# A third buffer for gate rows, earlier weight loads with one staging tile less, and splits behind the activations, in a fused attention, MLP and mixture-of-experts kernel

## The chip, the cores and the metric

The kernel runs on one core of a Trainium2 chip. The metric is the time of one execution in microseconds (us) of device time; several runs are taken and their median is what counts. The engines are named as in the profile: PE (TensorE, matmuls), PEld (its weight loads), DVE (VectorE), ACT (ScalarE), POOL (GpSimd) and SP (SyncE, which here issues nearly all DMAs, in the order of its own queue).

## The reference

Three stages follow each other. Attention over 8 batches and 8 heads, with 576 queries and with keys and values averaged in groups of 8, so that 72 are left. A dense MLP over the 4608 tokens. A mixture of 8 experts in which each token goes to the one expert with the largest logit.

```
k_p = mean of 8 neighbouring k;  v_p = mean of 8 neighbouring v
x = softmax(q @ k_p.T / sqrt(64)) @ v_p              # 4608 tokens x 512
x = ELU(x @ w_in) @ w_out                            # 512 -> 2048 -> 512
e = argmax(x @ w_gate);  g = softmax(x @ w_gate)[e]
out[token] = g * (relu(x @ w1[e]) @ w2[e])           # 512 -> 1024 -> 512
```

## The kernel before, in words

**Precision.** Every large product is made of three matmuls on fp32 values that are rounded to a high part (`xh`, `wih`, `gh`, `m1h`) and a remainder (`xl`, `wil`, `gl`, `m1l`). Whatever goes into a matmul is therefore first *split*: ACT casts the high part, DVE subtracts it (`split`, L118 to L120; `w_hi` L232 and `w_lo` L235 for the weights of the dense MLP).

**First stage.** Tokens stand in 12 blocks of 384 (three tiles of 128). The list `steps` holds one step for each block and each of 16 pieces of the 2048 inner columns; blocks 0 and 1 are interleaved at the start. `step(n)` issues the first product of its piece (`g1_mm`, L449, tile `h`), its ELU (ACT at L459 to L461, DVE at L466 and L467, then the split into `gh` on ACT at L473 and `gl` on DVE at L474), and the second product of an earlier piece (`g2`, L491, tiles `y`). Between these it runs named slots ("pre", "pe_mid", "dve_first", "bits", "act_end", "end" and others), which calls of `at(n, slot, function, ...)` have filled: attention of later blocks (`sp` L377, `mx` L386, softmax L395 to L401, transposes `aTp` L407 and their copies `aT` L413, `pv` L422, its split `xh`/`xl` L435/436), the pooling of keys and values on DVE (`kT`, `v` at L282), the weights of the dense MLP (bits of the mantissa L215 to L221, then `w_hi`, `w_lo`). This program order is also each engine's order. A few pieces at the start are on POOL: `w_lo` of the second and third weight chunks, and half of the pooling of the second batch's keys (`prep_k_pool`). Ten matmuls on a tile of zeros (`warm`, L279) stand in step 1.

**Gate logits.** For a finished block, DVE multiplies each of its three token tiles with each of the 8 gate rows (`r_logit`, L542, output `junk`). A gate row is loaded by SP and repeated over 128 partitions (`r_gate_load`, L535, tile `wgb`, 256 KB); two such tiles take turns, and after the third logit of expert e the row of expert e + 2 is requested. Then come `r_top`, `r_weight` (which also writes the block's rows to `ybuf` in DRAM with three DMAs, L589), `r_count` and `r_put` (the scatter of token numbers, L617).

**Second stage (from about 986 us).** Work items of 512 (D), 256 (S), 128 (T) and 32 (U) tokens of one expert follow each other: D0 to D7, then smaller ones; each is cut into 4 units, one for each 256 inner columns. `mix(n)` handles unit n: first product `m_g1` (L1159, tile `mhD`, 48 matmuls of 256 columns), transposes of rows for the next item (L1090), the second product of the unit before (`m_g2`, L1190, 24 matmuls of 512 columns), `m_act` (ACT relu into `hhD` L1171, DVE remainder `hlD` L1172), outputs, and last a list of "chores": logits of the last block in mix 0 to 3, `r_top` and `r_weight` of it in 4 and 5, then the lists of tokens by expert (`lists_rest` in 8, `lists_part` in 9 to 12). At mix 13 SP reads numbers that these lists have produced and fetches token indices for three more items (`m_index`, L1043 to L1050).

**Weights of the second stage.** `ahead(n)` is a small planner with planned times (10.2 us for each D unit). It issues the two loads of a unit (`m_load`: `w1st` L1115 and `w2st` L1122, 512 KB each, on SP) when the unit is needed within LOAD_REACH = 25 planned us, and its split (`m_split`: two casts and two subtractions, L119 and L120) when it is needed within SPLIT_REACH = 25, as far as tiles are free. The raw weights go through five staging tiles (`staged`, list `free_s`), two for each D unit. In `mix(n)` `ahead(n)` is called twice: once ahead of `m_g2` and `m_act`, once behind `m_out`.

Of the kernel before, what the change touches and what calls it, by code (L numbers as in the profile page):

```python
# [9 lines left out]
F32 = mybir.dt.float32  # L10
# [8 lines left out]
P = 128  # L19
B, H, S, D = 8, 8, 576, 64  # L20
POOLW = 8
SP = S // POOLW
DM = H * D
# [23 lines left out]
LOAD_REACH = 25  # L47
# [8 lines left out]
C_W = C_TRI + P  # L56
C_BASE = C_W + NE
C_TOK = C_BASE + NE
C_S = C_TOK + NT
# [29 lines left out]
def fused_kernel(ctx: ExitStack, tc: tile.TileContext, q, k, v, w_in, w_out, w_gate, w1, w2, cst, out):  # L89
# [17 lines left out]
    wge, basee, tokid, sidx = const(C_W, NE), const(C_BASE, NE), const(C_TOK, NT), const(C_S, NS)  # L107
# [62 lines left out]
    def wgb_tile(name):  # L170
        return ring(mrpool, [P, DM], F32, "wgb", 2, name)
# [62 lines left out]
    def w_lo(n, c, eng=None):  # L234
        (eng or nc.vector).tensor_sub(w_half(n, c, 1), decs.pop((n, c)).bitcast(F32), w_half(n, c, 0))  # L235
        if f"dec{n}_{c}" in slot_w:
            w_free(f"dec{n}_{c}")

    tri_st = w_tile([P, P], F32, "tri_st")
# [3 lines left out]
    def load_small():  # L243
        nc.sync.dma_start(tri_st, cst[:, C_TRI:C_TRI + P])
# [3 lines left out]
    def copy_small():  # L248
        nc.gpsimd.tensor_copy(tri, tri_st)
        w_free("tri_st")  # L250
        nc.gpsimd.tensor_copy(toki, tokid)
# [44 lines left out]

    def prep_k_pool(b, pr):
        st = kst.pop((b, pr)).rearrange("p (n j) -> p n j", j=POOLW)
        t = w_tile([P, SP, POOLW // 2], F32, f"kp{b}_{pr}")
        nc.gpsimd.tensor_add(t, st[:, :, 0:4], st[:, :, 4:8])  # L300
        nc.gpsimd.tensor_add(t[:, :, 0:2], t[:, :, 0:2], t[:, :, 2:4])
        nc.gpsimd.tensor_add(kTs[b % 2][:, pr].unsqueeze(2), t[:, :, 0:1], t[:, :, 1:2])
        w_free(f"kst{b}_{pr}", f"kp{b}_{pr}")
# [383 lines left out]
    for n, t in enumerate(range(TB, 2 * TB)):  # L687
# [9 lines left out]
        if n == 0:  # L697
            at(1, "pe_mid", warm, 10)
            at(1, "pe_mid", w_free, "zeros")
        for hh in range(2):  # L700
            at(n + 1, "act_hi" if n else "act_first", t_copy, t, hh, (nc.scalar.copy, nc.vector.tensor_copy)[hh])
        at(n + 1, "pe_end", pv_mm, t)
        at(n + 1, "copies", pv_copy, t)
    for pr in range(2, 4):
        at(0, "bits", prep_k, 1, pr)
    at(0, "bits", k_scale, 1)
# [3 lines left out]
    for n in range(2):  # L710
        w = n + 1
        at(n, "dve_first" if n == 0 else "bits", w_bits, w, 0)
        at(n, "act_hi" if n == 0 else "act_mid", w_hi, w, 0)
        at(n, "act_end" if n == 0 else "act_mid", w_lo, w, 0, nc.gpsimd)
        m, slot = (1, "act_first") if n == 0 else (n, "act_end")
        at(m, slot, w_bits, w, 1)
# [802 lines left out]
```

## Time and profile before

| | us |
|---|---|
| median of 3 runs | 1478.14 |
| lowest and highest run | 1475.92, 1480.35 |
| the profiled execution | 1484.07 |
| its span | 1482.3 |

| engine | busy us in the span |
|---|---|
| PE | 1414.8 (95%) |
| DVE | 967.1 (65%) |
| ACT | 740.9 (50%) |
| POOL | 146.0 (10%) |

The profile describes the one execution of 1484.07 us; what lies outside its span is the difference to 1482.3. Busy time is time in which an engine works on an instruction; an idle time in a row's square brackets is what the engine waited just ahead of that row, with the instruction that ended the wait. PEclk is the share of TensorE's full clock (2.4 GHz) that was granted in a stretch: 1.00 is all of it, 0.50 the lower level (1.2 GHz).

### The profile page before, as it was taken

How to read it: one execution, taken by the hardware profiler on the slowest of the kernel's cores; microseconds unless marked ns; L12 is line 12 of the kernel's file. 1: busy time of each engine (PE TensorE's matmuls, PEld its weight loads, DVE VectorE, ACT ScalarE, POOL GpSimd, SP SyncE). 2: the span in 40 equal slices, each digit the busy share in tenths (PEclk: the TensorE clock that was granted, in tenths of full speed). 3: DMA queues.
4: the chain of work that ended last, by engine and by line, in shares of the span. 5: the costliest groups of instructions: out<-in, count | busy, mean ns of one | idle time of the engine just before them, and what ended most of it. 6: DMA issues, size and time to landing. Idle time of an engine off the chain costs nothing. (4 is left out here: it accounts for less than half of the span.)

```text
span 1482.3 us, 24237 instructions
## 1 busy us (share of the span) xinstructions
PE 1414.8 (95%) x8842; PEld 1243.7 (84%) x8844; DVE 967.1 (65%) x2229; ACT 740.9 (50%) x1778; POOL 146.0 (10%) x139
## 2 busy tenths in 40 slices
PE   8699999999999999999999999998989799999998
PEld 5599778877888888888888888997879699888887
DVE  6899878796686768677768575974546343334351
ACT  5577665464555655556555655551233133324351
POOL 3100000000000000000000000111122121122110
PEclk8899999999999999999999999999999899999999
DMA  9234322734325251443333322454573417766660
GB/s 287 93 135 171 111 85 62 108 96 60 63 73 67 68 85 48 52 97 59 90 64 70 43 50 37 123 132 112 132 158 108 162 64 271 250 204 210 220 222 27
DMA packets 104417, 169.38 MB, mean 114 GB/s; under 512 B 14621, under 2 KB 45855, under 8 KB 104288
## 3 DMA queue, kind: packets, MB, share of 16 engines
q1 hardware_dynamic: 96880, 147.77, 38.9%
q0 software_dynamic: 7408, 19.97, 4.1%
q8 instruction: 71, 1.16, 0.4%
q14 instruction: 58, 0.48, 0.2%
HBM read 146.28 MB, written 21.88 MB: 113 GB/s over the span
## 5 line engine op out<-in xcount | busy, mean ns | idle before, releaser
L491 PE MATMUL y<-woh,gh 128*128 128x512 f32 x576 | 235.1, 408 | 1.5 <-ACT yr L507 1.4
L491 PE MATMUL y<-wol,gh 128*128 128x512 f32 x576 | 228.5, 397 | 0.0
L491 PE MATMUL y<-woh,gl 128*128 128x512 f32 x576 | 228.4, 396 | 0.0
L466 DVE SCALAR_TENSOR_TENSOR g<-g,th 128x384 f32<-128x384 f32 x192 | 106.5, 555 | 131.1 <-ACT th L461 130.4
L542 DVE SCALAR_TENSOR_TENSOR junk<-yr,wgb 128x512 bf16<-128x512 f32 x264 | 181.1, 686 | 12.8 <-DMA wgb<-in_moe_w_gate_dram 9.9
L449 PE MATMUL h<-xh,wih 128*128 128x384 f32 x768 | 171.2, 345 | 5.4 <-DVE g L467 3.8
L459 ACT ACTIVATE th<-h 128x384 f32<-128x384 f32 x192 | 94.3, 491 | 158.0 <-PE h L449 152.0
L473 ACT CAST gh<-g 128x384 fp32r<-128x384 f32 x192 | 98.8, 515 | 141.3 <-DVE g L467 117.9
L449 PE MATMUL h<-xl,wih 128*128 128x384 f32 x768 | 166.8, 339 | 0.0
L449 PE MATMUL h<-xh,wil 128*128 128x384 f32 x768 | 166.1, 338 | 0.0
L449 PEld LDWEIGHTS h<-xh,wih 128*128 128x128 f32 x768 | 137.6, 190 | 25.7 <-DVE g L467 4.9
L449 PEld LDWEIGHTS h<-xh,wil 128*128 128x128 f32 x768 | 137.8, 190 | 0.0
L449 PEld LDWEIGHTS h<-xl,wih 128*128 128x128 f32 x768 | 137.7, 190 | 0.1
L474 DVE TENSOR_TENSOR gl<-g,gh 128x384 fp32r<-128x384 f32 x192 | 109.0, 568 | 42.3 <-ACT gh L473 37.9
L491 PEld LDWEIGHTS y<-woh,gl 128*128 128x128 f32 x576 | 108.7, 189 | 26.1
L617 POOL DMA_INDIRECT tab<-toki,rpi x36 | 38.8, 1079 | 908.4 <-DVE rpi L615 483.7
L491 PEld LDWEIGHTS y<-woh,gh 128*128 128x128 f32 x576 | 108.7, 189 | 22.4 <-ACT yr L507 1.8
L1172 DVE SCALAR_TENSOR_TENSOR hlD<-mhD,hhD 128x512 fp32r<-128x512 f32 x64 | 43.8, 690 | 125.8 <-ACT hhD L1171 107.5
L491 PEld LDWEIGHTS y<-wol,gh 128*128 128x128 f32 x576 | 108.9, 189 | 17.6
L1171 ACT ACTIVATE hhD<-mhD 128x512 fp32r<-128x512 f32 x64 | 37.8, 597 | 166.8 <-PE myD L1190 158.4
L467 DVE TENSOR_TENSOR g<-g,h 128x384 f32<-128x384 f32 x192 | 106.4, 554 | 6.6
L1159 PE MATMUL mhD<-zhD,m1hD 128*128 128x256 f32 x512 | 85.9, 291 | 24.3 <-DVE hlD L1172 24.2
(276 smaller groups left out, 2502.4 us busy)
## 6 DMA issues: line engine op xcount, KB each, us to landing
wgb<-in_moe_w_gate_dram SPq DMA_DIRECT2D x96, 256.0 KB
w1stD<-in_moe_w_dram SPq DMA_DIRECT2D x32, 512.0 KB
w2stD<-in_moe_w_dram SPq DMA_DIRECT2D x32, 512.0 KB
kst<-in_k_dram SPq DMA_DIRECT2D x32, 288.0 KB
qT<-in_q_dram SPq DMA_DIRECT2D x36, 256.0 KB
ybuf<-yr SPq DMA_DIRECT2D x33, 256.5 KB
raw<-in_moe_w_in_dram SPq DMA_DIRECT2D x16, 512.0 KB
raw<-in_moe_w_out_dram SPq DMA_DIRECT2D x15, 512.0 KB
```

The costliest lines, as they stand in the source:

```text
L449: mark["g1"] = nc.tensor.matmul(ps, wi[i][a][:, c, o:o + P], bb[blk][:, c, :], start=n == 0, stop=n == 3 * KC - 1).ins
L459: nc.scalar.activation(th, hps[blk, f], AF.Relu, scale=-1.0)
L466: nc.vector.scalar_tensor_tensor(g, g, 1.0, th, op0=ALU.add, op1=ALU.mult)
L467: nc.vector.tensor_max(g, g, hps.pop((blk, f)))
L473: nc.scalar.copy(gh, g)
L474: nc.vector.tensor_sub(gl, g, gh)
L491: nc.tensor.matmul(ys[blk][j], a[:, js], wo[i][bb][:, o, :], start=n == 0 and f in FIRST[blk], stop=n == 2 and f in LAST[blk],)
L542: nc.vector.scalar_tensor_tensor(junk, yrows[blk][j][:, :DM], 1.0, pes[blk, e], op0=ALU.mult, op1=ALU.mult, accum_out=lgs[blk][:, j, e:e + 1])
L617: nc.gpsimd.indirect_dma_start(out=tab[:, :], out_offset=bass.IndirectOffsetOnAxis(ap=pi[:, j:j + 1], axis=0), in_=toki[:, TB * blk + j:TB ...
L1159: mark["g1"] = nc.tensor.matmul(ps[:, o], a[:, c, o * P:(o + 1) * P], x[:, c], start=k == 0, stop=k == len(terms) - 1).ins
L1171: nc.scalar.activation(hh, ps, AF.Relu)
L1172: nc.vector.scalar_tensor_tensor(hl, ps, 0.0, hh, op0=ALU.max, op1=ALU.subtract)
```

## The change

There are four parts.

- **Gate rows.** `wgb` has three tiles in place of two. Rows 0 to 2 of a block are requested ahead of its logits, and after expert e the row of e + 3.
- **Second stage.** LOAD_REACH goes from 25 to 36. The staging tiles go from five to four (`free_s` begins with one tile). The first call of `ahead(n)` in `mix(n)` goes; the one behind `m_out` stays.
- **Index block.** The three `index(x, m_index)` of mix 13 go from its start to its end.
- **Start.** `prep_k_pool` goes, and DVE pools all four parts of the second batch's keys at the end of step 0. All `w_lo` are on DVE. The ten warm matmuls of step 1 go. Constants and the slots of a few pieces (`t_copy`, `w_bits`, `w_hi`) are rearranged.

Lines of the changed kernel are some 8 to 15 smaller: L535 becomes L527, L1115 becomes L1101, L1122 becomes L1108, L1171 becomes L1157.

```diff
-LOAD_REACH = 25
+LOAD_REACH = 36
...
     def wgb_tile(name):
-        return ring(mrpool, [P, DM], F32, "wgb", 2, name)
+        return ring(mrpool, [P, DM], F32, "wgb", 3, name)
...
-    def prep_k_pool(b, pr):
...
-        if n == 0:
-            at(1, "pe_mid", warm, 10)
-            at(1, "pe_mid", w_free, "zeros")
...
-    for pr in range(2, 4):
-        at(0, "bits", prep_k, 1, pr)
-    at(0, "bits", k_scale, 1)
+    for pr in range(4):
+        at(0, "end", prep_k, 1, pr)
+    at(0, "end", k_scale, 1)
...
-        at(n, "act_end" if n == 0 else "act_mid", w_lo, w, 0, nc.gpsimd)
...
-        at(m, slot, w_lo, w, 1, nc.gpsimd)
+        at(n, "dve_first", w_bits, w, 0)
+        at(n, "act_hi", w_hi, w, 0)
+        at(n, "bits", w_bits, w, 1)
+        at(n, "bits", w_lo, w, 0)
+        at(n, "act_end", w_hi, w, 1)
+        at(n, "act_end", w_lo, w, 1)
...
         at(n0 - 2, "end", r_gate_load, blk, 1)
+        at(n0 - 1, "end", r_gate_load, blk, 2)
...
-            if j == TB - 1 and e + 2 < NE:
-                at(n0 + n, "end", r_gate_load, blk, e + 2)
+            if j == TB - 1 and e + 3 < NE:
+                at(n0 + n, "end", r_gate_load, blk, e + 3)
...
-    free_s, slot_s = [0, 1], {}
+    free_s, slot_s = [0], {}
...
     def mix(n):
         k, i = seq[n]
         it = main[k]
-        if n == 13:
-            for x in range(KD, KD + 3):
-                index(x, m_index)
         if n:
             m_g1(it, i)
         for it2, u in trans_at.get(n, ()):
             turn_rows(it2, u)
         if n:
-            ahead(n)
             k0, i0 = seq[n - 1]
             m_g2(main[k0], i0)
...
         ahead(n)
         for fn, *args in chores.pop(n, ()):
             fn(*args)
+        if n == 13:
+            for x in range(KD, KD + 3):
+                index(x, m_index)
```

Three places show how instructions move. The first is SP's queue as the second stage begins; `wgb11_4` is the row of expert 4 for the last block, `w1stD1_0` and `w2stD1_0` are the raw weights of unit 0 of item D1. Before:

```order
L535 DMA wgb11_4_10720<-in_moe2_w_gate_dram 128x512
L535 DMA wgb11_5_10728<-in_moe2_w_gate_dram 128x512
L1108 TENSOR_LOAD l7w_9771
L1108 ISA x2
L1115 ISA
L1115 DMA w1stD1_0_10789<-in_moe2_w1_dram 128x4x256
L1122 ISA
L1122 DMA w2stD1_0_10791<-in_moe2_w2_dram 128x2x512
L535 DMA wgb11_6_10839<-in_moe2_w_gate_dram 128x512
```

With the change:

```order
L527 DMA wgb11_3_10603<-in_moe2_w_gate_dram 128x512
L527 DMA wgb11_4_10611<-in_moe2_w_gate_dram 128x512
L1094 TENSOR_LOAD l7w_9756
L1094 ISA x2
L1101 ISA
L1101 DMA w1stD1_0_10708<-in_moe2_w1_dram 128x4x256
L1108 ISA
L1108 DMA w2stD1_0_10710<-in_moe2_w2_dram 128x2x512
L527 DMA wgb11_5_10718<-in_moe2_w_gate_dram 128x512
```

The loads of D1's first unit stood behind the row of expert 5 and stand now behind the row of expert 4. The loads of D2's first unit (`w1stD2_0`) stood behind the three DMAs to `ybuf` of the last block and stand now ahead of them.

The second is ACT's queue a little later; `hhD0_2` are the activations of unit 2 of D0, `m1hD1_0` and `m2hD1_0` the casts of D1's unit 0, `zhD1_0` a cast of transposed rows. Before:

```order
L1171 ACTIVATE hhD0_1_0_10706<-mhD0_1_0_10628 128x512
L1171 ACTIVATE hhD0_1_1_10710<-mhD0_1_1_10653 128x512
L119 CAST m1hD1_0_10793<-w1stD1_0_10789 128x1024
L119 CAST m2hD1_0_10797<-w2stD1_0_10791 128x1024
L1171 ACTIVATE hhD0_2_0_10825<-mhD0_2_0_10730 128x512
L1171 ACTIVATE hhD0_2_1_10829<-mhD0_2_1_10755 128x512
L1101 CAST zhD1_0_10906<-zTD1_0_10901 128x4x128
L1101 CAST zhD1_0_10906<-zTD1_1_10913 128x4x128
```

With the change:

```order
L1157 ACTIVATE hhD0_1_0_10691<-mhD0_1_0_10613 128x512
L1157 ACTIVATE hhD0_1_1_10695<-mhD0_1_1_10638 128x512
L1157 ACTIVATE hhD0_2_0_10802<-mhD0_2_0_10728 128x512
L1157 ACTIVATE hhD0_2_1_10806<-mhD0_2_1_10753 128x512
L119 CAST m1hD1_0_10814<-w1stD1_0_10708 128x1024
L119 CAST m2hD1_0_10818<-w2stD1_0_10710 128x1024
L1087 CAST zhD1_0_10893<-zTD1_0_10888 128x4x128
L1087 CAST zhD1_0_10893<-zTD1_1_10900 128x4x128
```

The casts of new weights stood ahead of the two activations of the same mix and stand now behind them. It is the same in every mix with a split, and DVE's subtractions move in the same way behind `hlD`.

The third is SP's queue at the index block; `l7T` and `l7D` are numbers that the lists produce, `oidxT0` is the last of the block's index fetches. Before:

```order
L1043 TENSOR_LOAD l7T_12045
L1043 ISA x2
L1050 REGISTER_ALU
L1050 DMA oidxT0_12255<-tab_64 128x1
L1115 ISA
L1115 DMA w1stD3_3_12308<-in_moe2_w1_dram 128x4x256
L1122 ISA
L1122 DMA w2stD3_3_12310<-in_moe2_w2_dram 128x2x512
L1108 TENSOR_LOAD l7w_9771
L1108 ISA x2
L1115 ISA
L1115 DMA w1stD4_0_12415<-in_moe2_w1_dram 128x4x256
```

With the change:

```order
L1101 ISA
L1101 DMA w1stD3_3_12140<-in_moe2_w1_dram 128x4x256
L1108 ISA
L1108 DMA w2stD3_3_12142<-in_moe2_w2_dram 128x2x512
L1094 TENSOR_LOAD l7w_9756
L1094 ISA x2
L1101 ISA
L1101 DMA w1stD4_0_12274<-in_moe2_w1_dram 128x4x256
L1108 ISA
L1108 DMA w2stD4_0_12276<-in_moe2_w2_dram 128x2x512
L1029 TENSOR_LOAD l7D_11748
L1029 ISA x2
```

The loads of D3's last unit and of D4's first stood behind the whole index block and stand now ahead of it. The load of D4's second unit (`w1stD4_1`) stands behind the index block in both.

## Rows read from the trace of the kernel before

**Rows 1.** Waits of TensorE (PE), 986 to 1482 us: us, times, longest.

```profile
PE mhD L1159 <- DVE hlD L1172: 24.2, 4, 10.8
```

**Rows 2.** Windows, line L1159 alone: stretch, its length, PE and PEld busy, PEclk, DMA share, GB/s.

```profile
1024.90:1032.60 7.70, 7.63 (x48) 7.57 (x48) 0.73 0.24 65
1052.30:1058.00 5.70, 5.67 (x48) 5.58 (x47) 1.00 0.25 101
1081.50:1089.90 8.40, 8.32 (x48) 8.22 (x48) 0.66 0.36 122
1177.70:1185.80 8.10, 8.01 (x48) 7.94 (x48) 0.69 0.79 274
```

**Rows 3.** Timeline of ACT, second stage: start, us, operation, [idle before <-releaser].

```profile
1020.71 1.04 ACT L119 CAST m1hD<-w1stD 128x1024 fp32r<-128x1024 f32 x1 [12.60 <-DMA w1stD<-in_moe_w_dram]
...
1173.02 1.04 ACT L119 CAST m1hD<-w1stD 128x1024 fp32r<-128x1024 f32 x1 [15.69 <-DMA w1stD<-in_moe_w_dram]
```

**Rows 4.** Timeline of SP's queue, 980 to 1170 us.

```profile
983.13 30.34 SPq L535 DMA_DIRECT2D wgb<-in_moe_w_gate_dram  x6
1014.30 0.40 SPq L1115 DMA_DIRECT2D w1stD<-in_moe_w_dram  x1
...
1067.96 0.39 SPq L1115 DMA_DIRECT2D w1stD<-in_moe_w_dram  x1
...
1169.51 0.39 SPq L1115 DMA_DIRECT2D w1stD<-in_moe_w_dram  x1
```

**Rows 5.** Waits of SP's queue, 986 to 1200 us.

```profile
SPq L1043 <- DVE more L1017: 34.5, 1, 34.5
...
SPq L589 <- DVE req L590: 27.0, 1, 27.0
```

**Rows 6.** Timeline of DVE at 1000 us.

```profile
1000.69 0.08 DVE L542 DVE_READ_ACCUMULATOR junk<-yr,wgb 128x1 f32 x1
```

**Rows 7.** Waits of DVE, 268 to 366 us.

```profile
DVE junk L542 <- DMA wgb<-in_moe_w_gate_dram: 14.2, 5, 4.0
DVE g L466 <- ACT th L461: 2.2, 3, 0.9
DVE gl L474 <- ACT gh L473: 1.4, 2, 0.7
```

**Rows 8.** Waits of TensorE, 268 to 366 us.

```profile
PE pv L422 <- ACT aT L413: 6.0, 3, 3.1
PE y L491 <- ACT yr L507: 1.4, 1, 1.4
```

**Rows 9.** Window over all engines: stretch, length, busy PE, PEld, DVE, ACT, POOL, then as above.

```profile
363.20:366.30 3.10, 3.09 (x21) 2.74 (x22) 2.83 (x15) 1.54 (x3) 0.00 (x0) 0.55 0.30 106
```

**Rows 10.** Timeline of SP's queue at 271 us.

```profile
271.48 2.79 SPq L535 DMA_DIRECT2D wgb<-in_moe_w_gate_dram  x1
```

**Rows 11.** Timeline of DVE at 274 us.

```profile
274.04 0.69 DVE L542 SCALAR_TENSOR_TENSOR junk<-part,wgb 128x512 bf16<-128x512 f32 x1 [2.58 <-DMA wgb<-in_moe_w_gate_dram]
```

**Rows 12.** Timeline of DVE, 38 to 68 us.

```profile
38.56 1.41 DVE L282 TENSOR_REDUCE kT<-kst 128x72 f32<-128x576 f32 x2
...
40.30 1.63 DVE L474 TENSOR_TENSOR gl<-g,gh 128x384 fp32r<-128x384 f32 x1
...
49.47 1.32 DVE L474 TENSOR_TENSOR gl<-g,gh 128x384 fp32r<-128x384 f32 x1 [1.10 <-ACT gh L473]
...
55.41 0.69 DVE L436 TENSOR_TENSOR xl<-pv,xh 128x512 fp32r<-128x512 f32 x1 [1.72 <-ACT xh L435]
...
64.69 0.68 DVE L235 TENSOR_TENSOR wol<-dec,woh 128x512 fp32r<-128x512 f32 x1
66.47 0.56 DVE L474 TENSOR_TENSOR gl<-g,gh 128x384 fp32r<-128x384 f32 x1 [1.10 <-ACT gh L473]
```

**Rows 13.** Timeline of GpSimd (POOL) at 40 us.

```profile
40.15 1.36 POOL L235 TENSOR_TENSOR wil<-dec,wih 128x512 fp32r<-128x512 f32 x1
```

**Rows 14.** Window over all engines, columns as in rows 9.

```profile
41.00:50.00 9.00, 5.62 (x61) 4.93 (x60) 7.73 (x13) 5.35 (x22) 3.00 (x3) 0.81 0.68 239
```

More of the change, by code (lines that the diff above doesn't have):

```diff
@@ L55 @@
 C_TRI = C_ID + P
-C_W = C_TRI + P
+C_TOK = C_TRI + P
+C_W = C_TOK + NT
 C_BASE = C_W + NE
-C_TOK = C_BASE + NE
-C_S = C_TOK + NT
+C_S = C_BASE + NE
 C_INC = C_S + NS
@@ L105, in const @@
         return small[:, at - C_W:at - C_W + n]
-    wge, basee, tokid, sidx = const(C_W, NE), const(C_BASE, NE), const(C_TOK, NT), const(C_S, NS)
+    wge, basee, sidx = const(C_W, NE), const(C_BASE, NE), const(C_S, NS)
     incl = const(C_INC, NE * NE).rearrange("p (a b) -> p a b", a=NE)
@@ L232, in w_hi, with w_lo @@
         nc.scalar.copy(w_half(n, c, 0), decs[n, c].bitcast(F32))
-    def w_lo(n, c, eng=None):
-        (eng or nc.vector).tensor_sub(w_half(n, c, 1), decs.pop((n, c)).bitcast(F32), w_half(n, c, 0))
+    def w_lo(n, c):
+        nc.vector.tensor_sub(w_half(n, c, 1), decs.pop((n, c)).bitcast(F32), w_half(n, c, 0))
         if f"dec{n}_{c}" in slot_w:
             w_free(f"dec{n}_{c}")
-    tri_st = w_tile([P, P], F32, "tri_st")
+    tri_st = w_tile([P, P + NT], F32, "tri_st")
     fill = w_tile([P, NTAB // P], I32, "fill")
@@ L243, in load_small @@
     def load_small():
-        nc.sync.dma_start(tri_st, cst[:, C_TRI:C_TRI + P])
+        nc.sync.dma_start(tri_st, cst[:, C_TRI:C_W])
         nc.sync.dma_start(tab.rearrange("(p n) o -> p (n o)", p=P), fill)
@@ L248, in copy_small @@
     def copy_small():
-        nc.gpsimd.tensor_copy(tri, tri_st)
+        nc.gpsimd.tensor_copy(tri, tri_st[:, :P])
+        nc.gpsimd.tensor_copy(toki, tri_st[:, P:])
         w_free("tri_st")
-        nc.gpsimd.tensor_copy(toki, tokid)
     vs = {}
@@ L295, in prep_k @@
             w_free(f"kst{b}_{pr}")
-    def prep_k_pool(b, pr):
[L298 to L303, printed above, removed]
     def k_scale(b):
@@ L696, in fused_kernel @@
             at(n + 1, "pe_mid", t_mm, t, hh)
-        if n == 0:
-            at(1, "pe_mid", warm, 10)
-            at(1, "pe_mid", w_free, "zeros")
-        for hh in range(2):
-            at(n + 1, "act_hi" if n else "act_first", t_copy, t, hh, (nc.scalar.copy, nc.vector.tensor_copy)[hh])
+            at(n + 1, "act_hi", t_copy, t, hh, (nc.scalar.copy, nc.vector.tensor_copy)[hh])
         at(n + 1, "pe_end", pv_mm, t)
         at(n + 1, "copies", pv_copy, t)
-    for pr in range(2, 4):
-        at(0, "bits", prep_k, 1, pr)
-    at(0, "bits", k_scale, 1)
+    for pr in range(4):
+        at(0, "end", prep_k, 1, pr)
+    at(0, "end", k_scale, 1)
     at(1, "end", v_tile, 1)
@@ L779, in step @@
         elu_a(blk, f)
-        run(n, "act_first")
         run(n, "act_hi")
@@ L889, in first_block @@
         pv_copy(2)
+        w_free("zeros")
         maxs(3)
@@ L892, in first_block @@
             w_load(3, c)
-        for pr in range(2):
-            prep_k_pool(1, pr)
         nc.sync.dma_start(small, cst[:, C_W:C_END])
@@ L1295, in fused_kernel @@
     at(n0 + 15, "end", r_put, last - 1)
-    for e in range(2):
+    for e in range(3):
         at(n0 + 15, "end", r_gate_load, last, e)
@@ L1371, in logits @@
             r_logit(last, e, j)
-            if j == TB - 1 and e + 2 < NE:
-                r_gate_load(last, e + 2)
+            if j == TB - 1 and e + 3 < NE:
+                r_gate_load(last, e + 3)
     chores = {n: [(logits, n)] for n in range(4)}
```

5 lines of the change are left out of this document (removed).

## The prediction

> **What bounds the kernel now.** TensorE is the busiest engine, so time can come only from where it stands still or runs at its lower clock. I read the waits of TensorE first, stage by stage. In the second stage nearly all of its idle time has one cause: its first product waits four times for `hlD`, 24.2 us in all, 10.8 at the longest [rows 1]. Next I read what comes behind a long wait. The same 48 matmuls of a first product keep TensorE busy for 5.67 us where the granted clock is 1.00, and for 7.63, 8.32 and 8.01 us behind the three long waits, where the clock is 0.66 to 0.73 on average, so part of each ran at the lower of the two levels, 1.2 GHz, [rows 2]. This costs 7.63 + 8.32 + 8.01 - 3 x 5.67 = 6.95 us more. The stalls are worth 24.2 + 7.0 = 31.2 us.
>
> The timeline of ACT tells why `hlD` is late. ACT sits idle for 12.60 us, and for 15.69 us in the worst case, in front of the cast of a new weight, waiting for the weight's DMA [rows 3]. The activations that `hlD` needs stand behind this cast in ACT's queue, though they don't use that weight. The timeline of SP tells why the DMA is late. In the first case its queue has the gate rows of the last block from 983.13 on, six issues that take 30.34 us because each row waits for a free tile, and the weight load goes out at 1014.30; ACT has it at 1020.71, 6.4 us later [rows 3, 4]. In the second, `w1st` leaves at 1067.96, behind three writes to `ybuf` that waited 27.0 us for DVE. In the third, it leaves at 1169.51, behind an index block that waited 34.5 us for the lists [rows 4, 5].
>
> In the first stage I read DVE's waits. From 268 to 366 us it waits 14.2 us in five goes for a gate row [rows 7]. A row goes out at 271.48 and DVE has it at 274.04, 2.6 us later, but its request comes after the logits of the tile that it replaces [rows 10, 11]. TensorE pays in the same stretch: `pv` waits 6.0 us and `y` 1.4 us for results that stand behind the stuck logit [rows 8], and after the longest of these waits 3.09 us of work run at a mean clock of 0.55 [rows 9].
>
> **The change part by part.**
>
> *Splits behind the activations.* Casts and subtractions of a new weight now follow the activations of their step on ACT and DVE. A late weight no longer holds `hlD` of its own step; it can hold only the next step's. That is a step of some 2 x 5.67 = 11.3 us away (an estimate: the second product streams as many columns as the first) [rows 2]. The work moved is the same on each engine.
>
> *Loads earlier.* LOAD_REACH 36 moves nearly every load up by a step. The load of D1's first unit now waits for the logits of expert 1, not expert 2: the third logit of expert 1 ends at 1000.69 [rows 6], so it goes out near 1001.5 and, with the 6.4 us above, lands near 1008, 12 us ahead of the time at which its cast ran before [rows 3]. D2's first unit goes ahead of the `ybuf` writes, D3's last and D4's first ahead of the index block. Each of the three loads that were late then lands before its split. I take all 31.2 us as gained; the bounds are 18.1 (the worst stall, 10.8 + 2.3, stays) and 31.2.
>
> *One staging tile less.* A load must wait for the split of two units before. Landing takes 6.4 us; the two casts of 1.04 us and the subtraction behind the second, which I take to be as long as a cast, take 3.1 [rows 3, 4]. Against these 9.5 us stand two steps, 22.6 us. I cost it at nothing; the cover is the 13.1 us between them, and without it each missing us is paid once in each of the 28 units of D1 to D7.
>
> *Index block at the end of mix 13.* What stands behind it now is the load of D4's second unit. The block still has to wait for the lists, but the split of that unit is planned more than a step behind the lists' end, and holds no activations of its own step. Cost nothing, bound 13.1 as above.
>
> *Third gate tile.* A row is asked for an expert earlier, at least three logits of 0.69 us [rows 11] plus the step's other DVE work ahead of its use, against 2.6 us. The rows stop being late. Gain: 7.4 us of TensorE's waits [rows 8] and 3.09 x 0.45 = 1.4 us of clock [rows 9], 8.8 together. What is late next is the ELU chain: DVE waits 2.2 + 1.4 us there for ACT in the same stretch [rows 7], and some of it grows as the rows stop covering it. I take 8.0, with bounds 0 and 8.8.
>
> *Start.* DVE gets two poolings at 0.7 us and four `w_lo` at 0.68 us: 1.4 + 2.7 = 4.1 us. It loses two slow instructions. `gl` takes 1.63 and 1.32 us while GpSimd runs a subtraction beside it, and 0.56 alone [rows 12, 13], so 1.07 + 0.76 = 1.8 us come back. The net 2.3 us fall where DVE is idle for 1.10 + 1.72 = 2.8 us waiting for ACT [rows 12]. I take a gain of 0.5. The bounds are a gain of 1.8 (all added work in idle time) and a loss of 2.3 (none of it). Removing ten warm matmuls frees TensorE at a time when it waits for DVE anyway. I cost their going at nothing, and weigh this as follows. From 41 to 50 us TensorE is busy 5.62 us at a granted clock of 0.81, with those matmuls in place just ahead [rows 14].
>
> The page "TensorE: Matmul & The Clock Gate" of the Trainium skill, section "Why this matters for your kernels", speaks against this: long idle gaps between bursts of matmuls throw the clock back to half, so without the warm matmuls what follows would run at the lower level. By it the sum would be up to 3.5 us higher; the row shows that the clock falls here even with them, so I take the sum without it.
>
> *The sum.* 1484.07 for the profiled execution, less 31.2, 8.0 and 0.5, is 1444.4. That execution is 5.9 us above the median of the runs shown (1478.14), so the forecast for the median is **1438 us**, 2.7% faster.
>
> **The rivals.**
>
> *A: slower, by the staging tiles.* Four tiles in place of five make each load wait for a split that was moved later. The point from which it decides is a landing time of 22.6 - 3.1 = 19.5 us; each us above is paid 28 times, so at 21.5 us the kernel would lose 56 and stand near 1438 + 56 = 1494. For it: in the window of the third stall the DMA share is 0.79 and 274 GB/s move [rows 2], so transfers can crowd. Against it: a weight landed in 6.4 us, and even in that crowd in 1173.02 - 1169.51 = 3.5 us [rows 3, 4].
>
> *B: one second-stage stall stays.* The index block still stands ahead of D4's second unit, and it waited 34.5 us before [rows 5]. If DVE's lists come later against TensorE's faster steps, its split, then the activations of the next step, wait as now. Price 10.8 + 2.3 = 13.1: 1451. Against it: the splits no longer stand ahead of the activations of their own step, so the wait has a step of slack.
>
> *C: the gate tile buys nothing in the middle.* DVE is busy there and TensorE's waits for `aT` could have come anyway. Price 8.0: 1446. Against it: `pv`'s waits lie in the stretch that holds five of the rows' waits.
>
> *D: the clock at the start.* With the warm matmuls gone, the 5.62 us of work at 0.81 would take 5.62 x 0.81 / 0.5 = 9.1 us, 3.5 more [rows 14]: 1441.5.
>
> **How the numbers follow.** The forecast gets 0.70: three stalls with one common cause, each with its late load in SP's queue, are the bulk of it. B gets 0.13, C 0.07, D 0.06, A 0.04. The range goes from 1430 (all of the bounds on the good side give 1484.07 - 5.9 - 31.2 - 8.8 - 1.8 = 1436.4, and the runs shown, 1475.92 to 1480.35, spread by a few us more) to 1457 (close to B with C, 1438 + 13.1 + 8.0 = 1459). A measurement of this kernel can tell about 0.3%, 4.4 us, from no change. Every case but A is faster by more. Of these I keep 0.02 for a milder form of A, which costs only as much as the rest gives: 0.94 faster, 0.02 within, 0.04 slower.
>
> **What would show it.** Right: the waits of TensorE for `hlD` fall from 24.2 to below 2 us, all first products of D items take 5.6 to 5.8 us, `w1st` of D1's first unit leaves SP near 1001 and the casts follow the activations without idle time for a DMA. DVE's waits for gate rows from 268 to 366 us fall below 2 us and TensorE's for `aT` and `yr` with them. At the start the row of `gl` is 0.56 us everywhere. Wrong: a wait of TensorE for `hlD` over 5 us in the second stage, ACT idle in front of a cast for a weight's DMA with TensorE idle behind it, DVE's waits for rows gone but TensorE's idle time in the middle still above 5 us, or waits of SP's queue for staging tiles that end later than the splits that need them.

## The result, and the profile after

The changed kernel takes 1433.22 us (median of 4 runs, 1432.44 to 1434.88) against 1478.39 for the kernel before: a ratio of 0.9697 with a 95% interval of 0.9680 to 0.9714, 45 us or 3.0% less. The forecast was 1438, in a range of 1430 to 1457. The two profiled executions, 1484.07 and 1434.88 us, lie 49.2 us apart; the one before was 5.7 us above its median and the one after 1.7, so some 4 us of that belong to the executions and not to the change.

TensorE's line of the page, after:

```profile
PE 1399.5 (98%) x8834; PEld 1236.8 (86%) x8834; DVE 968.3 (68%) x2235; ACT 739.9 (52%) x1778; POOL 132.3 (9%) x129
```

It was busy 1414.8 us in a span of 1482.3 and is now busy 1399.5 in 1433.1. The span lost 49.2 us, of which idle time is 33.9 and busy time 15.3. Of the busy time 2.3 us are the ten warm matmuls that went; most of the rest is the same work that runs quicker. The forecast had 7.0 and 1.4 us of this kind, and this is the part that was too small.

**The second stage.** TensorE's waits in it, after (compare [rows 1]):

```profile
PE mhD L1145 <- DVE hlD L1158: 0.9, 1, 0.9
```

The 24.2 us for `hlD` are 0.9. First products after the change, in the same columns as [rows 2]:

```profile
987.90:993.70 5.80, 5.72 (x48) 5.62 (x48) 1.00 0.27 96
...
1012.10:1017.90 5.80, 5.76 (x48) 5.70 (x48) 1.00 0.44 131
```

They run at the full clock and take 5.72 and 5.76 us, where three took 7.63 to 8.32. Over the whole stage the same 3147 matmuls keep TensorE busy 460.31 us before and 453.36 after. SP's queue shows what became of the late loads (compare [rows 4]):

```profile
963.50 18.01 SPq L527 DMA_DIRECT2D wgb<-in_moe_w_gate_dram  x5
982.34 0.40 SPq L1101 DMA_DIRECT2D w1stD<-in_moe_w_dram  x1
...
1123.19 0.37 SPq L1101 DMA_DIRECT2D w1stD<-in_moe_w_dram  x1
...
1126.29 0.34 SPq L1036 DMA_DIRECT2D oidxD<-tab  x1
...
1135.94 0.39 SPq L1101 DMA_DIRECT2D w1stD<-in_moe_w_dram  x1
```

The gate rows ahead of D1's first load are five, not six, and hold the queue 18.01 us, not 30.34. The load leaves at 982.34; the second stage begins 19.6 us earlier here (first `hhD` at 969.89, not 989.46), so that on the old scale this is 1001.9, where the forecast had 1001.5. D4's first unit leaves at 1123.19, ahead of the index block, and D4's second at 1135.94 behind it. ACT then finds its weights there:

```profile
999.19 0.60 ACT L1157 ACTIVATE hhD<-mhD 128x512 fp32r<-128x512 f32 x1 [2.20 <-PE myD L1176]
999.68 1.04 ACT L119 CAST m1hD<-w1stD 128x1024 fp32r<-128x1024 f32 x1
```

The activation comes first, the cast follows it with no idle time. ACT's waits for weight DMAs, 12.60 and 15.69 us in [rows 3], are gone from the stage.

**The middle.** DVE's waits (columns as in [rows 7]) and TensorE's (as in [rows 8]), 264 to 357 us after:

```profile
DVE g L458 <- ACT th L453: 5.8, 6, 1.6
DVE gl L466 <- ACT gh L465: 2.2, 5, 0.7
DVE junk L534 <- DMA wgb<-in_moe_w_gate_dram: 0.2, 1, 0.2
```

```profile
PE pv L414 <- ACT aT L405: 0.5, 2, 0.3
```

DVE's wait for rows falls from 14.2 to 0.2 us. Its waits for the ELU grow from 3.6 to 8.0, as the forecast expected of work that the rows had covered, and they cost TensorE next to nothing: it waits 0.5 us in place of 8.5 (6.0 and 1.4 in [rows 8], and 1.1 for `h`). The whole stretch in windows (columns as in [rows 9]), before and after:

```profile
265.10:372.60 107.50, 98.86 (x602) 85.40 (x601) 82.67 (x225) 55.94 (x153) 7.57 (x6) 0.98 0.49 83
```

```profile
264.20:360.20 96.00, 95.51 (x602) 84.47 (x601) 82.94 (x224) 56.40 (x152) 6.62 (x6) 1.00 0.50 90
```

The same 602 matmuls keep TensorE busy 98.86 us before and 95.51 after; the mean clock was 0.98 and is 1.00.

**Where the time went, by steps.** ACT's first ELU instruction of a step is a good mark, since each of the 192 steps has one. Steps 3, 43, 63, 98, 107 and 191 and the first `hhD` of the second stage, before:

```profile
66.87 0.49 ACT L459 ACTIVATE th<-h 128x384 f32<-128x384 f32 x1
...
265.10 0.49 ACT L459 ACTIVATE th<-h 128x384 f32<-128x384 f32 x1 [1.07 <-PE h L449]
...
372.58 0.49 ACT L459 ACTIVATE th<-h 128x384 f32<-128x384 f32 x1 [0.95 <-PE h L449]
...
540.63 0.49 ACT L459 ACTIVATE th<-h 128x384 f32<-128x384 f32 x1
...
588.01 0.49 ACT L459 ACTIVATE th<-h 128x384 f32<-128x384 f32 x1 [1.87 <-PE h L449]
...
985.01 0.49 ACT L459 ACTIVATE th<-h 128x384 f32<-128x384 f32 x1
...
989.46 0.60 ACT L1171 ACTIVATE hhD<-mhD 128x512 fp32r<-128x512 f32 x1 [2.86 <-PE mhD L1159]
```

and after:

```profile
65.80 0.49 ACT L451 ACTIVATE th<-h 128x384 f32<-128x384 f32 x1 [0.84 <-PE h L441]
...
264.21 0.49 ACT L451 ACTIVATE th<-h 128x384 f32<-128x384 f32 x1 [1.07 <-PE h L441]
...
360.21 0.49 ACT L451 ACTIVATE th<-h 128x384 f32<-128x384 f32 x1 [0.91 <-PE h L441]
...
527.23 0.49 ACT L451 ACTIVATE th<-h 128x384 f32<-128x384 f32 x1
...
571.03 0.49 ACT L451 ACTIVATE th<-h 128x384 f32<-128x384 f32 x1 [1.86 <-PE h L441]
...
965.37 0.48 ACT L451 ACTIVATE th<-h 128x384 f32<-128x384 f32 x1
...
969.89 0.60 ACT L1157 ACTIVATE hhD<-mhD 128x512 fp32r<-128x512 f32 x1 [2.92 <-PE mhD L1145]
```

| stretch | before, us | after, us | difference |
|---|---|---|---|
| up to step 3 | 66.87 | 65.80 | -1.1 |
| steps 3 to 43 | 198.23 | 198.41 | +0.2 |
| steps 43 to 63 | 107.48 | 96.00 | -11.5 |
| steps 63 to 98 | 168.05 | 167.02 | -1.0 |
| steps 98 to 107 | 47.38 | 43.80 | -3.6 |
| steps 107 to 191 | 397.00 | 394.34 | -2.7 |
| first `hhD` to the end of the span | 492.84 | 463.21 | -29.6 |

The rows of steps 63 to 98 and 107 to 191 were not in the forecast at all.

**The start.** With subtractions on DVE alone, `gl` takes 0.55 us at 40.65, where it took 1.63 beside GpSimd [rows 12, 13]:

```profile
40.65 0.55 DVE L466 TENSOR_TENSOR gl<-g,gh 128x384 fp32r<-128x384 f32 x1
```

TensorE now waits 5.92 us for the pooled keys, and much of what follows runs at the lower clock; the window of [rows 14] has a clock of 0.58, not 0.81:

```profile
44.85 1.23 PE L369 MATMUL sp<-kT,qT 64*64 64x72 f32 x28 [5.92 <-DVE kT L299]
```

```profile
41.00:50.00 9.00, 5.04 (x49) 4.17 (x50) 8.83 (x17) 5.84 (x24) 0.00 (x0) 0.58 0.67 224
```

The page "TensorE: Matmul & The Clock Gate" of the Trainium skill, section "Why this matters for your kernels", says that long idle gaps between bursts of matmuls throw the clock back to half. The trace agrees: from 44 to 52 us, behind the wait of 5.92 us, the granted clock is 0.50. (Whether this comes from the warm matmuls that went is another matter: warm_back, below.) It doesn't show in the time: step 3 comes 1.1 us earlier, not later, 0.8 of it counted from the first `h`. DVE is busy 8.83 of the 9.00 us of this window, so I read the stretch as DVE's.

### The profile page after: what moved, and what is told of

Read it like the earlier page. It is cut to its first block, busy times and chain, and to the rows that moved or that the text cites. A ratio compares the mean times of both kernels' runs of the same rounds, so it can differ in the third digit from the quotient of the medians.

```text
span 1433.1 us, 24197 instructions
## 1 busy us (share of the span) xinstructions
PE 1399.5 (98%) x8834; PEld 1236.8 (86%) x8834; DVE 968.3 (68%) x2235; ACT 739.9 (52%) x1778; POOL 132.3 (9%) x129
## 5 line engine op out<-in xcount | busy, mean ns | idle before, releaser
L441 PE MATMUL h<-xl,wih 128*128 128x384 f32 x768 | 167.3, 340 | 0.0
L1157 ACT ACTIVATE hhD<-mhD 128x512 fp32r<-128x512 f32 x64 | 38.2, 598 | 218.3 <-PE myD L1176 197.5
L453 ACT ACTIVATE th<-th 128x384 f32<-128x384 f32 x192 | 100.8, 525 | 6.1
```

Source lines behind the costliest of these rows:

```text
L441: mark["g1"] = nc.tensor.matmul(ps, wi[i][a][:, c, o:o + P], bb[blk][:, c, :], start=n == 0, stop=n == 3 * KC - 1).ins
L453: nc.scalar.activation(th, th, AF.Tanh, scale=-0.5)
L1157: nc.scalar.activation(hh, ps, AF.Relu)
```

## The experiments

Twelve kernels were run, on three chips, each beside the kernel before on the same chip. On these chips the kernel before took 1482.75, 1480.95 and 1482.81 us. The table gives, for each profiled execution, the stretches of the table above that matter, and the median of all runs of that kernel.

| kernel | steps 43 to 63 | 63 to 98 | 98 to 107 | 107 to 191 | second stage | median | ratio to before (95%) |
|---|---|---|---|---|---|---|---|
| before | 107.48 | 168.05 | 47.38 | 397.00 | 492.84 | 1478.39 | |
| after | 96.00 | 167.02 | 43.80 | 394.34 | 463.21 | 1433.22 | 0.9697 (0.9680 to 0.9714) |
| order_only | 106.76 | 168.04 | 45.80 | 398.24 | 476.61 | 1464.64 | 0.9884 (0.9839 to 0.9930) |
| reach_only | 112.43 | 168.05 | 45.78 | 397.65 | 463.55 | 1453.51 | 0.9799 (0.9757 to 0.9841) |
| index_only | 105.22 | 168.05 | 47.14 | 397.11 | 479.49 | 1469.48 | 0.9922 (0.9894 to 0.9950) |
| four_tiles | 109.94 | 168.05 | 43.99 | 397.49 | 494.09 | 1483.22 | 1.0010 (0.9980 to 1.0040) |
| gates_only | 96.00 | 167.01 | 44.81 | 394.33 | 492.16 | 1465.96 | 0.9901 (0.9882 to 0.9919) |
| no_start | 95.98 | 166.99 | 47.09 | 394.70 | 459.48 | 1429.72 | 0.9659 (0.9641 to 0.9677) |
| warm_back | 96.31 | 167.31 | 43.53 | 394.34 | 460.22 | 1428.44 | 0.9642 (0.9627 to 0.9657) |
| trans_late | 96.47 | 166.99 | 43.81 | 394.34 | 460.29 | 1428.19 | 0.9644 (0.9627 to 0.9660) |
| shift_only | 106.95 | 167.10 | 44.48 | 396.31 | 495.51 | 1481.33 | 0.9991 (0.9966 to 1.0016) |
| shift_1024 | 104.63 | 167.11 | 45.27 | 394.36 | 495.18 | 1479.61 | 0.9980 (0.9952 to 1.0008) |
| after_again | 96.60 | 167.02 | 43.80 | 394.34 | 462.67 | 1431.58 | 0.9653 (0.9620 to 0.9686) |
| late_and_warm | 96.31 | 167.29 | 43.81 | 394.33 | 462.12 | 1431.12 | 0.9650 (0.9617 to 0.9683) |

### Which edit cures the second stage

**order_only**, the splits behind the activations and nothing else:

```diff
         if n:
-            ahead(n)
             k0, i0 = seq[n - 1]
             m_g2(main[k0], i0)
```

> The kernel before with one edit: the first call of the weight planner in each mix goes, so that splits follow the activations; loads, staging tiles, index block, gate tiles and start stay. Theory (a late weight does harm only because its split stands ahead of the activations of its own step): TensorE's waits for hlD fall from 24.2 to under 3 us although the weights still land late, first products no longer run at the lower clock, and the time falls by about 29 us, to 1447 to 1452. Rival (the late load is the cause; the order only moves the stall to the next step): at least two of the three stalls stay, 15 to 24 us of waits for hlD, and the time falls by less than 12 us.

TensorE's waits in the second stage:

```profile
PE mhD L1159 <- DVE hlD L1172: 6.7, 3, 3.4
PE zTD L1090 <- DVE rpe L611: 2.6, 1, 2.6
```

SP's queue and ACT's waits in the same kernel:

```profile
979.98 30.32 SPq L535 DMA_DIRECT2D wgb<-in_moe_w_gate_dram  x6
1011.14 0.40 SPq L1115 DMA_DIRECT2D w1stD<-in_moe_w_dram  x1
```

```profile
ACT m1hD L119 <- DMA w1stD<-in_moe_w_dram: 25.6, 5, 7.6
```

Neither theory holds as it was put. The weights come as late as before (the load leaves 31.2 us behind the first gate row, as it did in [rows 4]), and ACT still waits 25.6 us for them, but no longer in front of the activations of the same step. The second stage falls by 16.2 us (492.84 to 476.61), 55% of what the whole change gives. Waits for `hlD` are 6.7 us in three places and one of 2.6 us for transposes is new. In each of the four places ACT had just waited for a late weight (3.44, 4.63, 7.62 and 7.09 us), and DVE's subtractions of that weight stand ahead of what TensorE waits for. At the index block, on ACT, DVE and TensorE:

```profile
1158.30 1.05 ACT L119 CAST m1hD<-w1stD 128x1024 fp32r<-128x1024 f32 x1 [7.62 <-DMA w1stD<-in_moe_w_dram]
...
1161.51 1.23 DVE L120 TENSOR_TENSOR m2lD<-w2stD,m2hD 128x1024 fp32r<-128x1024 f32 x1 [0.90 <-ACT m2hD L119]
...
1163.39 0.74 PE L1159 MATMUL mhD<-zhD,m1hD 128*128 128x256 f32 x4 [1.82 <-DVE hlD L1172]
```

`hlD` of the next step follows the subtraction at 1162.66 us, and TensorE has waited 1.82 us for it. The longest wait, 3.4 us, is at 1358.85 us, among the smaller items, long behind the three stalls. So the order takes most of the harm out of a late load, and not all.

**reach_only**:

```diff
-LOAD_REACH = 25
+LOAD_REACH = 36
```

> The kernel before with one edit: LOAD_REACH 36 instead of 25; splits stay ahead of the activations. Theory that the late loads are the cause: the loads of D1's and D2's first units and of D3's last leave SP earlier than the gate row, the ybuf writes and the index block that held them, waits for hlD fall below 6 us, and the time falls by 24 to 30 us, to 1448 to 1454. Rival (the order of splits is what matters, and loads are held by other things in SP's queue as well): waits for hlD stay above 12 us and the time falls by less than 15 us. If this run and the one with the order alone both give the whole, either of the two edits is enough.

```profile
PE mhD L1159 <- DVE hlD L1172: 1.8, 1, 1.8
```

The theory was right: one wait of 1.8 us is left, and the second stage takes 463.55 us, 0.3 more than in the changed kernel. This one number is nearly the whole second-stage gain. The six kernels with all edits of the second stage lie between 459.48 and 463.21 there, so that the order of the splits and the place of the index block, with the loads in time, have some 4 us at most left to cure, and no stall.

**index_only**, the index block moved as in the change:

```diff
-        if n == 13:
-            for x in range(KD, KD + 3):
-                index(x, m_index)
         if n:
             m_g1(it, i)
...
         for fn, *args in chores.pop(n, ()):
             fn(*args)
+        if n == 13:
+            for x in range(KD, KD + 3):
+                index(x, m_index)
```

> The kernel before with one edit: the index block of mix 13 goes from its start to its end. Theory: only the third stall goes (10.8 us of waiting and 2.3 us of lower clock), the first two stay with 6.0 and 6.5 us; the time falls by about 13 us, to 1465. Rival: the block then stands ahead of the load of D4's first unit, whose split still stands ahead of the activations of mix 14, so that the stall moves one step on; the time falls by less than 5 us.

```profile
PE mhD L1159 <- DVE hlD L1172: 13.9, 4, 6.3
```

The waits fall from 24.2 to 13.9 us, with the first two of the long ones still there (6.3 is the longest), and the second stage falls by 13.4 us (492.84 to 479.49). The third stall was the index block's, as read from SP's queue, and its price, 13.1 by the forecast, was right. The stall did not move on to D4's first unit.

**four_tiles**:

```diff
-    free_s, slot_s = [0, 1], {}
+    free_s, slot_s = [0], {}
```

> The kernel before with one edit: four staging tiles instead of five. Theory: landing (6.4 us) and split (3.1 us) fit into two steps of 11.3 us, so nothing changes: within 4 us of 1478. Rival (loads wait for tiles, and each us over is paid in 28 units): more than 12 us slower, with waits of TensorE for hlD in many more than four places.

```profile
PE mhD L1159 <- DVE hlD L1172: 23.6, 4, 10.4
```

The four waits are the four of before. A staging tile less costs nothing that can be measured (0.9980 to 1.0040). That holds with late loads; with early ones no run has five tiles and all else as in the change, but there TensorE waits only 0.9 us for `hlD` in all, so that a missing tile can't cost much.

### What the gate tile gives

**gates_only**: the kernel before with `wgb` at three tiles, rows asked for at e + 3, four staging tiles, and the constants rearranged to make room:

```diff
-        return ring(mrpool, [P, DM], F32, "wgb", 2, name)
+        return ring(mrpool, [P, DM], F32, "wgb", 3, name)
...
-                at(n0 + n, "end", r_gate_load, blk, e + 2)
+                at(n0 + n, "end", r_gate_load, blk, e + 3)
...
-    free_s, slot_s = [0, 1], {}
+    free_s, slot_s = [0], {}
```

> The kernel before with the third gate tile (rows asked for three experts ahead), the four staging tiles and the small constants that make room for it; order of splits, LOAD_REACH, index block and start as before. Theory (late gate rows cost TensorE idle time and clock in the first stage): DVE's waits for gate rows go, the steps from 265 to 369 us take 11 to 12 us less and those from 540 to 585 us 3 to 4 less, the second stage keeps its three stalls; 14 to 16 us faster than before. Rival (DVE is busy there and TensorE's waits for aT come anyway): less than 6 us.

TensorE's waits from 260 to 370 us, and from 960 us on:

```profile
PE pv L422 <- ACT aT L413: 0.5, 2, 0.3
```

```profile
PE mhD L1160 <- DVE hlD L1173: 26.6, 3, 10.1
```

Steps 43 to 63 take 96.00 us, as in the changed kernel to the hundredth. All seven kernels with two gate tiles lie between 104.63 and 112.43 there, all seven with three between 95.98 and 96.60. The third tile takes out 8.0 us in the least favourable pairing and 16.5 in the most, and also the spread. The two other edits in this kernel leave the stretch long when they come alone (109.94 in four_tiles, 106.95 in shift_only). The second stage keeps its stalls. The median is 15.0 us below before, as expected, but part of the expectation was wrong: the 3 to 4 us of steps 98 to 107 are not the gate tile's. Two kernels with two tiles are as quick there (43.99 and 44.48) and one with three is slow (47.09). What differs most there is the time from step 99 to step 100, 6.3 to 9.2 us: ACT stands idle ahead of `th`, 4.68 us in no_start and 1.75 in the changed kernel, with the same instructions around it, and in no_start `h` has been done for some 3 us by then. What ACT waits for the profile doesn't show, and the cause stays open.

### The start

**no_start** is the changed kernel with the start of before (the part of the change's diff from `prep_k_pool` to the `w_lo` of step 1 undone). **warm_back** is the changed kernel with the ten warm matmuls in step 1 again:

```diff
             at(n + 1, "pe_mid", t_mm, t, hh)
+            if n == 0 and hh == 1:
+                at(1, "pe_mid", warm, 10)
+                at(1, "pe_mid", w_free, "zeros")
```

> The changed kernel with the start of before: pooling half on GpSimd, subtractions of the first weights on GpSimd, ten warm matmuls in step 1. Theory (the new start is worth next to nothing: DVE bounds it both ways, and what it saves in slow DVE instructions it pays in added ones): within 2 us of the changed kernel. Rival one (the new start gains by freeing DVE from GpSimd): 1.5 us or more slower than the changed kernel, and a longer time from the first h to the ELU of step 3. Rival two (the new start loses, by the clock without the warm matmuls): 2 to 3.5 us faster than the changed kernel.

> The changed kernel with the ten warm matmuls put back into step 1, and nothing else. Theory (TensorE waits there for DVE): the granted clock from 44 to 52 us rises, but the ELU of step 3 comes at the same time within 1 us and the total stays within 2 us. Rival (the lower clock behind the idle time costs): 2 to 3.5 us faster.

no_start is at 1429.72 us and warm_back at 1428.44, on the same chip; the changed kernel was at 1433.22 and 1431.58 on two others. By ratio to before, the changed kernel is at 0.9697 and 0.9653, so that two measurements of it differ by more than it does from either of these. What decides is the first 32 us: up to the first `h` the program is the same in trans_late and warm_back. Their windows from 20 to 32 us:

```profile
20.00:32.00 12.00, 10.46 (x81) 8.22 (x82) 8.37 (x14) 4.33 (x8) 0.17 (x1) 0.60 0.96 318
```

```profile
20.00:32.00 12.00, 10.19 (x101) 8.78 (x102) 11.18 (x20) 7.56 (x26) 0.26 (x1) 1.00 0.96 321
```

TensorE was granted a mean clock of 0.60 there in one execution and 1.00 in the other. The same 16 matmuls of `pv` take 1.98 us in the one and 1.09 in the other, and the first `h` starts at 31.65 and at 28.26 us. It starts between 31.3 and 32.2 us in five of the fourteen executions and between 27.9 and 29.2 in nine, and both happen with either start. Counted from the first `h` to the ELU of step 3, the old start takes 33.9 to 35.6 us in nine executions (mean 34.7), the new one 34.5, 34.7 and 34.1 in three (after, trans_late, after_again). The means differ by 0.3 us, which is less than the spread, so that no gain of the new start is shown. With the warm matmuls back it is 32.8 and 34.1 us (warm_back, late_and_warm).

My expectation that the clock would rise with the warm matmuls was wrong for the work that it was about. From 44 to 52 us it is 0.61 in warm_back and 0.50 in the changed kernel, but warm_back's work stands some 3 us earlier. The ten matmuls stand ahead of the wait for the pooled keys; this wait is still 3.86 us long, and the 28 matmuls behind it take 1.23 us as in the changed kernel:

```profile
41.10 1.23 PE L369 MATMUL sp<-kT,qT 64*64 64x72 f32 x28 [3.86 <-DVE kT L299]
```

In no_start, where GpSimd pools half of these keys, TensorE doesn't wait for them, the clock from 41 to 50 us is 1.00, and 32 such matmuls take 0.73 us. So in the new start the clock falls behind the wait for DVE's pooling, and the warm matmuls don't prevent it. The old start isn't free of the lower clock either (0.51 from 41 to 50 us in order_only). No claim on the start is larger than the spread between executions.

### Two edits beyond the change

**trans_late** moves the transposes of attention tiles 6 and 8 behind the second product of their steps, where TensorE still waited:

```diff
-    OUT = {6: 27}
+    OUT = {6: 27, 7: 29}
...
-            at(n, "pe_mid", t_mm, t, hh)
-            at(n, "act_mid", t_copy, t, hh, nc.scalar.copy)
+            at(n, "pe_end" if t in (6, 8) else "pe_mid", t_mm, t, hh)
+            at(n, "act_end" if t in (6, 8) else "act_mid", t_copy, t, hh, nc.scalar.copy)
...
+        if t == 8 and True:
+            at(n + 1, "pe_mid", pv_mm, t)
+            at(n + 1, "act_mid", pv_copy, t)
+            return
```

> The changed kernel with the transposes of attention tiles 6 and 8 moved behind the second product of their steps (and the products with v of tiles 7 and 8 one step later), where TensorE still waits: 2.4 us at 165, 1.6 at 187, 1.7 at 199 us, with the lower clock behind two of them. Theory: these waits and some 2 to 3 us of lower clock go, 5 to 8 us less than the changed kernel. Rival (ACT and DVE are late there and the wait only moves to the next step): less than 2 us.

TensorE's waits from 150 to 240 us in the changed kernel, and in this one:

```profile
PE aTp L399 <- ACT g L452: 2.4, 1, 2.4
PE pv L414 <- ACT aT L405: 2.1, 2, 1.6
PE aTp L399 <- DVE s L393: 1.7, 1, 1.7
```

```profile
PE sp L369 <- ACT aT L405: 3.6, 1, 3.6
PE sp L369 <- DVE xl L428: 1.3, 1, 1.3
```

The transposes hardly wait any more (0.4 us), but the scores of the next tile now wait 3.6 us for a copy of `aT` and 1.3 for `xl`. Steps 3 to 43 take 197.74 us, 0.7 less than in the changed kernel and as many as in after_again (197.77): the rival was right.

**late_and_warm** has this edit and that of warm_back, and after_again is the changed kernel beside it:

> The changed kernel with both small edits: transposes of attention tiles 6 and 8 behind the second product of their step, and the ten warm matmuls back in step 1. Theory: the two don't overlap in time, so their gains add: 4 to 8 us less than the changed kernel in the same call. Rival (what each seemed to gain was the state of the first 32 us): within 2 us of it.

> The changed kernel once more, beside the others of this call: 1432 to 1435 us where its first h comes near 31.5 us, 1428 to 1431 where it comes near 28.3 us (the first 32 us run at either of two clocks in different executions of unchanged code).

1431.12 against 1431.58 on the same chip: the gains don't add, and the rival was right here too. The profiled execution of after_again has its first `h` at 27.95 us and took 1430.63, as expected. None of these variants can be told from the changed kernel, which stays the best version that was shown.

### The steps that nobody had touched

Steps 63 to 98 hold no wait of TensorE in either kernel, yet they took 168.04 or 168.05 us in five kernels and 166.99 to 167.31 in the others. What parts them is one small edit, the token numbers taken out of the tile `small`, which makes room for the gate tile. It makes a tile of constants 144 bytes smaller in each partition, and in the built program all 32 weight slots move down by 128 bytes, to multiples of 2048. **shift_only** is that edit alone on the kernel before; **shift_1024** has an unused tile of 1024 bytes ahead of the slots as well (the first line, which shift_only doesn't have):

```diff
+    cpool.tile([P, 256], F32, name="spare_row")
...
-    tri_st = w_tile([P, P], F32, "tri_st")
+    tri_st = w_tile([P, P + NT], F32, "tri_st")
...
-        nc.gpsimd.tensor_copy(toki, tokid)
+        nc.gpsimd.tensor_copy(toki, tri_st[:, P:])
```

> The kernel before with the small edit of the constants alone (token numbers taken from the staged constants, so that a tile of constants is 144 bytes a partition smaller); it moves all 32 weight slots down by 128 bytes, to addresses that are multiples of 2048. In the runs so far every kernel with this edit takes 167.0 us from step 63 to 98 and 394.3 to 394.7 from 107 to 191, every one without it 168.05 and 397.0 to 398.2. Theory (the addresses make the second products of the dense MLP quicker): 167.0 and 394.4 here too, stalls and gate waits as before, 4 to 6 us less in all. Rival (the third gate tile does it): 168.05 and 397.0 to 398.2, and no change in the time.

> The same as the run with the shift alone, with an unused tile of 1024 bytes a partition ahead of the weight slots, so that each begins 1024 bytes behind a multiple of 2048. Theory one (a row of 512 fp32 values must not cross a multiple of 2048): the stretch from step 63 to 98 takes 168.05 us as in the kernel before. Theory two (any multiple of 1024 will do): 167.0. If the run with the shift alone shows no gain, neither is told apart.

Groups of one product each of the dense MLP, 372 to 540 us, by form: mean ns is the last number ahead of the second bar. Before, with the shift alone, and with 1024 more:

```profile
L491 PE MATMUL y<-wol,gh 128*128 128x512 f32 x105 | 41.5, 395 | 0.0
...
L449 PE MATMUL h<-xh,wil 128*128 128x384 f32 x141 | 30.3, 336 | 0.0
```

```profile
L491 PE MATMUL y<-wol,gh 128*128 128x512 f32 x106 | 41.5, 392 | 0.0
...
L449 PE MATMUL h<-xh,wil 128*128 128x384 f32 x144 | 30.9, 335 | 0.0
```

```profile
L492 PE MATMUL y<-wol,gh 128*128 128x512 f32 x107 | 41.9, 392 | 0.0
```

The second product's matmuls, which stream 512 columns out of a weight slot, take 395 ns on average before and 392 in both; the first product's, which stream token tiles against weights that were loaded, 336 and 335. The step time follows: 168.05 to 167.10 and 167.11. By the starts in the trace, the matmuls of the second product follow each other 2.3 to 4.1 ns closer on average in these 35 steps with the shift, which adds up to 0.94 us; those of the first product don't. In steps 107 to 191 TensorE is busy 396.60 or 396.61 us in all five kernels without the edit and 394.33 to 394.45 in all nine with it. The rest of these steps' time is a wait of `pv` that goes back to a late gate row: 1.9 us with the shift alone, 0.4 before.

So this edit does it and the gate tile doesn't, and slots at 1024 behind a multiple of 2048 do as well as slots on one. That it is the address of the streamed weights is read from this and not shown alone: in the built programs `gh` and `gl`, which the second product reads as well, keep their addresses with the shift alone, while some token tiles moved by the same 128 bytes, and no run has the edit with the slots left where they were. In the total, 1481.33 against 1482.81 (0.9966 to 1.0016), this can't be told from the spread between executions; the 4 to 6 us that I expected are not shown.

## Why the prediction was right, and where it was off

**The second stage** was forecast at 31.2 us and gave 29.6. Of these 6.95 are busy time (460.31 to 453.36), to the hundredth what the three slow first products had been costed at, which is luck as far as the last digits go; the other 22.7 are idle time, for which the forecast had 24.2. Over the kernels of the table the stage takes 494.0 us on average without its edits (five) and 461.3 with all of them (six), 32.6 less. The reading was right in each of the three places: which load was late, what in SP's queue held it, and that ACT's casts passed the wait on. What the forecast did not part was which of the edits would do it. It gave the credit to splits and loads together; by reach_only, the earlier loads do nearly all of it alone (29.3 us), and by order_only the splits would have given 16.2 without them. "It can hold only the next step's" is what order_only shows; but "a step of some 11.3 us" is not enough of a cover for loads that leave as late as before, and TensorE still waits 1.6, 2.6 and 1.8 us where the gate rows, the writes to `ybuf` and the index block hold them. That the changed kernel has 0.9 us of such waits left is mostly the work of the earlier loads.

**The staging tile** was rightly costed at nothing, as far as four_tiles shows, and rival A had no part in it.

**The index block** had the right price (13.4 against 13.1, where stages that no edit touched differ by up to 3.4), and rival B did not come: D4's second unit loads at 1135.94, and no wait of TensorE for `hlD` follows.

**The middle** is the mis-sized term: 8.0 us forecast, 11.5 measured. Idle time gave 8.0 (6.0 + 1.4 in [rows 8] and 1.1 for `h` in the same view, against 0.5 after) where the forecast counted 7.4 and then took 0.8 off the sum for an ELU chain that would come to light. That chain did come to light, on DVE, and TensorE didn't wait for it. The other 3.4 us (98.86 to 95.51) are TensorE's work running quicker. The forecast had 1.4 for the lower clock, from one window of 3.1 us [rows 9]; the clock of the whole stretch, 0.98 over 107.5 us, is worth some 2 by my estimate, and the shift of the weight slots some 0.6 more (1.0 in 168 us, from steps 63 to 98); what is left is within the rounding of the clock. Rival C did not come: in gates_only the stretch takes 96.00 us.

**The constants** were not in the sum at all: their rearrangement was taken for an edit without effect. By the two runs with the shift it gave 1.0 us in steps 63 to 98 and 2.2 in steps 107 to 191 (the rest of the 2.7 there is a wait that goes back to a gate row), in stretches where TensorE is hardly ever idle.

**The start** was forecast at a gain of 0.5 us; it gave 1.1 in the two profiled executions, and over twelve of them the means differ by 0.3, within their spread. Rival D's clock came (0.58, not 0.81), but, by warm_back, not for want of the warm matmuls: it falls behind a wait of 5.92 us for the pooled keys, which the forecast didn't see, and with the matmuls back it falls too. Its 3.5 us did not come; DVE is busy nearly all of that stretch, and as I read it the slower work of TensorE lies in time that it would have waited.

**The sum.** 31.2 + 8.0 + 0.5 = 39.7 forecast. Replacing the terms by what was measured, without the stretch whose cause is open (steps 98 to 107), gives 29.6 + 11.5 + 1.0 + 2.7 + 0.3 = 45.1. That this meets the difference of the medians, 45.2, is luck: most of these terms come from one execution of each kernel, and on another chip the changed kernel was 51.2 us below before (1431.58 against 1482.81). With the means over the kernels, 32.6, 11.4, 1.0, 3.1 and 0.3, the sum is 48.4.

## What to carry to other kernels

Where an engine's queue is in order, ask of every wait what stands behind it that doesn't need what is waited for; then ask which is easier, to move the waiting instruction or to start the transfer a step earlier, for the earlier transfer alone may be worth nearly all (29.3 us here, of 29.6 to 33.4) and the reorder only part of it (16.2). When the busiest engine has no idle time, an edit that merely moves tiles in memory need not be free of effect: compare the mean duration of one form of matmul before and after. And a gain of a microsecond or two at the start can't be read from one execution, when unchanged code ahead of it differs by three.

## What the runs showed of the hardware that was not expected

- The matmuls of 512 columns out of weight slots take 395 ns on average in the kernels whose slots begin 128 bytes behind a multiple of 2048, and 392 in those where they begin on such a multiple or 1024 behind it (`wol,gh` in the groups above); 35 steps take 168.05 us in the one case and 167.0 to 167.3 in the other.
- Up to the first `h` the same instructions run at different mean clocks in different executions (0.60 and 1.00 from 20 to 32 us in two of them; the same 16 matmuls take 1.98 and 1.09 us), and the first `h` comes some 3 us later in the one.
- Waits of TensorE that go can bring back more than themselves: in steps 43 to 63, 8.0 us less of idle time came with 3.4 us less of busy time for the same 602 matmuls (some 0.6 of it, by an estimate from steps 63 to 98, the shift of the slots).
- Ten warm matmuls ahead of a wait of 3.86 us did not keep the clock up behind it: the same 28 matmuls take 1.23 us with them and without them (there behind 5.92 us).
